# Sliding-window attention beside a GELU MLP on one core: the five channel tiles of each chunk's products added into one, not two, ahead of the logit matmuls, under a new order of pieces

## The chip, the cores and the metric

The kernel runs on one core of one Trainium2 chip. The metric is device microseconds (us) of one execution; lower is better. A core has a matrix engine (TensorE, PE in the profile, with PEld for its weight loads), a vector engine (VectorE, DVE), a scalar engine (ScalarE, ACT), GpSimd (POOL) and SyncE (SP). POOL and SP mostly issue DMA transfers here. Each engine works through its own instructions in program order; semaphores make one engine wait for another or for a transfer.

## The reference, cut to what matters

```
x  = A_x                                   # 1 x 2048 x 640, bf16
xn = layernorm(x)
q, k, v = split(xn @ wqkv)                 # 32 heads of 20 channels each
# position s looks at the 8 positions s, s-2, ..., s-14 (masked below 0)
logits = einsum("bhsd,bhswd->bhsw", q, kg) * scale
attn   = softmax(logits)
o      = einsum("bhsw,bhswd->bhsd", attn, vg)
mlp    = gelu(xn @ w1 + b1) @ w2 + b2      # hidden size 1536
out    = x + o @ wo + mlp
```

## The kernel before, in words

The 2048 positions are cut into four chunks of 512 columns, a chunk into four blocks j of 128. Activations lie with channels on the 128 partitions: 640 channels are five channel tiles of 128. The weights of q, k and v are read in strides, so that a partition holds channels of one head only in all five tiles: four partitions belong to each of the 32 heads.

For each chunk n, the steps are these. Each has a short name, a piece, which the written order uses; n is the first digit and j or an output tile the next.

- Layer norm: statistics (`st`, or `su`, `sq`, `ng` on ACT for chunks 2 and 3), `rs`, `rc`, then `xn`; transposes through PE for chunk 0 (`tp`, copied out by `tc`) and by DMA from SP for the others (`tc` there is L292).
- Projections on PE: `pj` n, which (0 q, 1 k, 2 v), tile (L336, five matmuls of 512 columns); chunk 0 has narrower ones (L349, L380, pieces `ga`, `gb`, `gd`, `ge`, `hj`). ACT copies each result out (`pc`, L400; `hc`, `gc` for chunk 0). `pad` copies 14 columns of the chunk before in front of k and v; for chunk 0 `pad01` and `pad02` are memsets on POOL (L405).
- Products q*k on DVE (`qk` n j h, L433): one instruction of 128x2560 makes, for block j, the products with four of the eight window positions (half h), for five channel tiles. They go to the SBUF tile `half`, of which there is one only, for all chunks.
- Adds of channel tiles on DVE (`pa` n j k, L465): k = 0 adds tiles 2 and 3 onto 0 and 1 (128x2048), k = 1 adds tile 1 onto 0 (128x1024). Two tiles, 0 and 4, are then left (`KEPT` is 2).
- Logits on PE (`lg`, L474): each matmul takes `head_of`, 128x32, as weights and sums the channels of each head over the partitions; the four blocks j write four groups of 32 partitions of one PSUM tile `L`. With two tiles left a chunk has 2 tiles x 2 halves x 4 blocks = 16 matmuls of 512 columns.
- Softmax: `cl` copies L to `Lb` (ACT, L486), `mask` (chunk 0), `m` and `mx` (DVE, L496 to L502), `ex` (ACT, L513, with a table load), `ss`, `ri`, `at` (DVE, L519 to L531).
- `xd` n j (SP, L548) spreads the weights of block j over the partitions by DMA. For odd chunks the target is the first half of `x_sb`, the input tile.
- Products with v (`av` n j h, DVE, L557), written into `half` again, so only after `lg` of the following chunk's logits where these were made in between; the sum of both halves (`aa`: an accumulating DMA from POOL for chunks 0 to 2, L567, an add on DVE for chunk 3, L569); two more adds (`ab`, L573, `ot`, L577).
- MLP: `f1` n_t (PE, L586) and `ge` n_t (ACT, L602), twelve each. Outputs `o` n block part (PE, L622 and L624, PSUM tiles `lo` and `hi`): parts 0 to 3 are the MLP's, part 4 is `wo` with the attention output `ot`. `oc` copies out (ACT), `od` adds to the output in DRAM (POOL, L635).
- Output base: `xp` (SP, L301) writes x to the output in DRAM: `xp0` chunk 0, `xp1` chunk 1, `xp2` chunks 2 and 3. `xb` n (POOL, L305) adds the bias b2 to chunk n there, after `xp` has landed.

The order is written out by hand as one string, `ORDER`, of these names. Walking it emits each engine's program; what stands in front of a piece on its engine runs before it. The order runs the chunks overlapped: the products q*k of chunk 1 come before the products with v of chunk 0, and so on. PE results of `f1`, `pj` and `hj` share four PSUM buffers, `psA`; a fifth waits until ACT has copied one out. A chunk's end is `ot33`, then `o334` and `ohi` on PE, two adds on DVE (`oclo`, L643, `ochi`, L652), and two stores.

Of the kernel before, what the change touches and what calls it, by code (L numbers as in the profile page):

```python
# [16 lines left out]
S, D, F, H, W, DIL = 2048, 640, 1536, 32, 8, 2  # L17
# [3 lines left out]
KT, FT = D // P, F // P  # L21
# [8 lines left out]
LASTB = S // P - 1  # L30
WARM = 10

KEPT = (2, 2, 2, 2)
BY_DMA = ((0, 1, 2, 3), (0, 1, 2, 3), (0, 1, 2, 3), ())
CUT = 2560
ACT_STATS = (2, 3)
# [1 line left out]
COLS = ((0, 2), (2, 4), (4, 5))  # L38

ORDER = """  # L40
wa ho st00a sum1 st00 rs00 rc00 neg1 sq1 xn00a tp00a wb xn00b tp00b mean1 tc00a rs01 rc01 tb b1 tc00b ga gb2 xn01 tp01
tc01a tc01b gb3 gb4 gd ge gc4 gc1 hj100 st02a st02 rs02 hc100 st03a st03 hj101 gc0 rc02 xn02 rs03 hj102 rc03 xn03
hc101 hc102 tp02 tc02 hj202 tp03 tc03 hj201 hc201 hj010 st11a hc010 st13a hc202 st12a hj012 hc012 hj112 hc112 f10_3
st11 ldx hj011 f10_9 st10a st10 st12 st13 rs1 qk011 ge0_3 rc1 xn13 pad01 qk000 qk001 tc13 ge0_9 xn12 tc12 pa000 qk010
pk hj110 hc110 hj111 hc111 hc011 qk030 qk031 qk021 pad11 xn11 f10_10 tc11 pa010 xn10 qk020 tc10 ge0_10 f10_2 ge0_2
hj200 hc200 f10_0 pa030 f10_6 f10_11 su20 ge0_6 xp2 su22 su23 pj111 pc111 ge0_0 su21 ng2 pj110 pc110 pj104 pc104 sq23
pj120 pc120 ge0_11 sq20 pj114 pc114 pj113 pc113 pa001 pa020 pa021 pj102 pc102 pa031 pa011 lg0 cl0 mask m0 hj212 hc212
pj123 pc123 mx0 ex0 pj103 pc103 pj112 pc112 ss0 ri0 pj101 pc101 pj100 pc100 qk110 qk100 ld2 ldo xb2 sq22 qk130 pj124
pc124 hj211 sq21 qk121 rs2 pj121 pc121 hj210 hc210 rc2 f10_8 qk131 hc211 f11_9 ge1_9 xp0 xn20 f10_1 ge0_1 f10_7 tc20
f11_5 xb0 qk120 xn21 tc21 qk101 ge1_5 ge0_7 xn23 tc23 ge0_8 xn22 qk111 o000 f11_8 ge1_8 pa130 at0 pa110 f11_0 ge1_0  # L50
pa100 pad12 f10_5 ge0_5 f11_3 ge1_3 f11_6 su32 tc22 pa120 pa101 xd00 f10_4 su33 pj214 pc214 pa111 su31 su30 pj210
pc210 pad21 xd02 ge0_4 pj211 pa121 ge1_6 pa131 lg1 pj200 pad02 av000 av001 aa00 pc200 ng3 sq32 sq31 sq30 av020 pc211
av021 xd01 av011 o001 pj213 pc213 pj122 pj202 pc202 av010 o002 ab00 ot00 pj204 pj212 o003 pc212 pj223 pj222 cl1 aa02
xd03 pc122 av030 av031 m1 mx1 sq33 rs3 pj201 rc3 pc204 o004 oc00 ab02 ot02 pj224 ex1 o020 aa01 aa03 ss1 ri1 xn33 at1
ab01 ot01 ab03 o021 o022 o023 o024 xp1 tc33 pc201 xn32 tc32 pc222 oc02 ot03 od02 f12_7 xd10 av101 pad22 xd12 pc223
f11_4 xn30 o030 o031 o032 o033 pc224 xd11 xn31 pj221 av100 aa10 o034 oc03 f11_2 o010 ge1_4 tc31 av120 o011 o012 o013
o014 av110 av111 aa11 ge2_7 pc221 od03 f11_7 ge1_7 pj203 pc203 ge1_2 xd13 f11_1 av131 tc30 pj311 pc311 av130 aa13
pj304 f12_3 ge2_3 pj310 pc310 pc304 ge1_1 pj302 av121 aa12 ab10 ot10 f11_10 pc302 ge1_10 pj313 pc313 qk201 qk200 pj312
pj314 ab11 ot11 qk210 pc312 oc01 od01 f13_8 ge3_8 qk211 o130 ab13 pa200 pc314 f11_11 ge1_11 qk231 f12_6 o131 ot13
qk230 xb3 f12_0 ge2_0 pj220 pc220 o132 o133 o134 oc13 pj301 pc301 pa210 ge2_6 ab12 ot12 qk221 pj300 pj324 pc300 qk220  # L60
f13_7 xb1 pc324 od13 pa211 pj303 o120 pa230 pa220 pa231 pc303 pad31 pa221 pa201 lg2 ge3_7 cl2 qk301 f12_2 m2 mx2 ex2
f13_10 f12_8 ge2_8 o121 o122 o123 od00 o124 oc12 qk310 ss2 pj320 pc320 qk311 ri2 at2 xd22 xd20 o110 o111 qk331 o112
o113 o114 oc11 od11 qk330 f13_6 ge3_6 f12_5 ge2_5 ge3_10 o100 ge2_2 qk320 pa330 qk321 pa320 f13_5 f12_4 ge3_5 pj322
f13_2 o101 ge2_4 qk300 xd21 pc322 pa321 o102 o103 o104 ge3_2 pa300 pa301 pa331 pa310 pa311 lg3 f13_3 av210 f13_9 oc10
od10 od12 av211 aa21 ge3_3 f12_10 ge2_10 xd23 av230 av200 f12_1 ge2_1 ge3_9 av231 aa23 f12_9 ge2_9 f13_1 ge3_1 f13_4
f12_11 av201 av221 ab21 ge3_4 av220 pj321 o210 o211 o212 f13_0 ot21 ge2_11 o213 o214 f13_11 cl3 m3 mx3 ex3 pad32 ss3
ri3 at3 xd32 oc21 o200 o201 pc321 o202 aa20 ab20 ot20 ab23 ot23 ge3_0 aa22 o203 o310 o204 oc20 pj323 pc323 ab22 ot22
av320 o230 o231 o232 o233 o234 od20 oc23 av321 aa32 xd30 o311 o312 od21 ab32 o220 o221 o222 o223 o224 ge3_11 xd31
av311 od23 o313 av301 av310 oc22 od22 o320 o321 o322 o323 av300 ot32 o324 oc32 aa31 ab31 ot31 o314 oc31 o300 o301 o302
xd33 od32 aa30 o330 o303 ab30 ot30 o304 av331 av330 aa33 ab33 o331 o332 o333 ot33 od31 xl o334 oclo oc30 ohi ochi ochd  # L70
od30
""".split()


# [1 line left out]
def kernel(  # L76
# [16 lines left out]
    nc = tc.nc  # L93
# [24 lines left out]
    wqkv = [wts.tile([P, KT, D], BF16, name=f"w{s}_sb") for s in "qkv"]  # L118
# [6 lines left out]
    wqkv_v = A_wqkv.rearrange("(t p) n -> p t n", p=P)  # L125
# [6 lines left out]
    def load_w(s):  # L132
        nc.sync.dma_start(wqkv[s][:], wqkv_v[:, :, s * D : (s + 1) * D])
# [2 lines left out]
    nc.vector.memset(x_sb[:, 1, 0:16], 0.0)  # L136
    nc.scalar.dma_start(x_sb[:, 1, :], x_nb[:, 1, :])
    nc.scalar.dma_start(b1_rt[0:FT, :], B_b1.rearrange("(t p) -> t p", p=P))
    load_w(0)
    load_w(1)  # L140
    load_x(2, BPC)
    load_w(2)
# [34 lines left out]
    mask = consts.tile([H, W, MW], BF16, name="mask")  # L177
# [289 lines left out]
    def do_lg(n):  # L467
        L = psL.tile([P, W, P], F32, tag="L", name="L")
        tiles["L", n] = L
        ts = {KT: range(KT), 3: (0, 1, 4), 2: (0, 4), 1: (0,)}[KEPT[n]]  # L470
        for t in ts:
# [189 lines left out]
    def piece(name, fn, *args):  # L661
        assert name not in pieces
        pieces[name] = lambda: fn(*args)
# [36 lines left out]
    for n in range(NCH):  # L700
# [27 lines left out]
        for j in range(BPC):  # L728
            for k in range({KT: 0, 3: 1, 2: 2, 1: 3}[KEPT[n]]):
                piece(f"pa{n}{j}{k}", do_pa, n, j, k)  # L730
# [57 lines left out]
```

## Time and profile before

| what | us |
|---|---|
| median of 3 runs | 207.31 (206.93 to 208.23) |
| the profiled execution, its time | 207.49 |
| its span, first to last instruction | 205.7 |
| PE busy in it | 200.8 |
| DVE busy in it | 175.4 |
| ACT busy in it | 127.7 |

The profile is of one execution. Its span leaves out 1.8 us of the execution's time (207.49 less 205.7). Busy time of PE is of pipelined matmuls that overlap: the distance from one start to the next says more. A group's row gives count, busy time, mean nanoseconds of one, and the idle time of the engine just before it with what ended it. The timeline gives start, duration, engine, line, operands, count, and in brackets the idle time before and what ended it.

### The profile page before, as it was taken

How to read it: one execution, taken by the hardware profiler on the slowest of the kernel's cores; microseconds unless marked ns; L12 is line 12 of the kernel's file. 1: busy time of each engine (PE TensorE's matmuls, PEld its weight loads, DVE VectorE, ACT ScalarE, POOL GpSimd, SP SyncE). 2: the span in 40 equal slices, each digit the busy share in tenths (PEclk: the TensorE clock that was granted, in tenths of full speed). 3: DMA queues.
4: the chain of work that ended last, by engine and by line, in shares of the span. 5: the costliest groups of instructions: out<-in, count | busy, mean ns of one | idle time of the engine just before them, and what ended most of it. 6: DMA issues, size and time to landing. Idle time of an engine off the chain costs nothing.

```text
span 205.7 us, 3262 instructions
## 1 busy us (share of the span) xinstructions
PE 200.8 (98%) x1285; PEld 112.2 (55%) x1285; DVE 175.4 (85%) x214; ACT 127.7 (62%) x242; POOL 34.4 (17%) x49
## 2 busy tenths in 40 slices
PE   7899999999999999999999999999999999999994
PEld 2797745565445555555555554555444555555552
DVE  3489999379998989949999994999979979799981
ACT  5488999899999879916466344834616854221210
POOL 2000000050000422102703303001023420311210
DMA  6999389969258599899996965018209998931244
GB/s 210 390 397 370 75 232 326 403 102 185 64 116 264 99 186 181 142 192 124 207 198 113 144 107 64 0 16 182 41 0 132 162 193 162 192 41 17 30 52 64
DMA packets 27335, 31.77 MB, mean 154 GB/s; under 512 B 9272, under 2 KB 22072, under 8 KB 27320
## 3 DMA queue, kind: packets, MB, share of 16 engines
q0 software_dynamic: 7408, 12.78, 39.4%
q1 hardware_dynamic: 19600, 18.58, 31.4%
q8 instruction: 10, 0.16, 0.3%
q10 hardware_dynamic: 312, 0.20, 0.3%
q14 instruction: 5, 0.04, 0.1%
HBM read 10.00 MB, written 7.54 MB: 85 GB/s over the span
## 4 chain that ended last, share of the span: by engine, by line
PE 95%; DMA 3%; SPq 0%; DVE 0%; issue 0%
PE lo L622 29%; PE hps L586 25%; PE pps L336 24%; PE hi L624 7%; PE gps L380 7%; DMA wq_sb<-in_A_wqkv_dram 3%; PE L L474 2%; PE gps L349 1%; PE tp L280 0%; SPq L130 0%; DVE osb L652 0%
## 5 line engine op out<-in xcount | busy, mean ns | idle before, releaser
L586 PE MATMUL hps<-xnT,w_sb 128*128 128x512 bf16 x240 | 55.6, 379 | 0.0
L433 DVE TENSOR_TENSOR half<-qT,kT 128x2560 bf16<-128x2560 bf16 x32 | 46.2, 1482 | 2.9 <-PE L L474 2.8
L622 PE MATMUL lo<-w_sb,hT 128*128 128x512 bf16 x144 | 41.3, 379 | 0.0
L586 PEld LDWEIGHTS <-w_sb 128*128 128x128 bf16 x240 | 22.9, 98 | 26.3 <-issue 0.8
L629 ACT CAST osb<-lo 128x512 bf16<-128x512 f32 x15 | 8.8, 587 | 36.8 <-PE hi L624 18.5
L624 PE MATMUL hi<-w_sb,hT 128*128 128x128 bf16 x144 | 31.5, 219 | 0.0
L602 ACT ACTIVATE hT<-hps,b1T 128x512 bf16<-128x512 f32 x36 | 24.0, 683 | 10.7 <-PE hps L586 10.7
L465 DVE TENSOR_TENSOR half<-half 128x2048 bf16<-128x2048 bf16 (+1 forms) x32 | 29.0, 952 | 0.2
L635 POOL DMA_DIRECT2D out_dram<-osb x15 | 13.6, 973 | 77.1 <-ACT osb L630 68.5
L557 DVE TENSOR_TENSOR half<-vT,x_sb 128x2560 bf16<-128x2560 bf16 x16 | 22.8, 1485 | 4.4 <-DMA x_sb<-e 3.0
L557 DVE TENSOR_TENSOR half<-vT,ax 128x2560 bf16<-128x2560 bf16 x16 | 22.8, 1485 | 2.3 <-PE L L474 1.4
L622 PEld LDWEIGHTS <-hT 128*128 128x128 bf16 x144 | 14.1, 98 | 16.8
L622 PE MATMUL lo<-wo,oT 128*128 128x512 bf16 x80 | 23.1, 379 | 0.0
L567 POOL DMA_DIRECT2D half<-half x12 | 14.3, 1195 | 48.9 <-DVE half L557 48.5
L336 PE MATMUL pps<-xnT,wv_sb 128*128 128x512 bf16 x75 | 18.5, 379 | 0.0
L336 PE MATMUL pps<-xnT,wq_sb 128*128 128x512 bf16 x75 | 18.3, 379 | 0.0
L336 PE MATMUL pps<-xnT,wk_sb 128*128 128x512 bf16 x75 | 17.7, 379 | 0.0
L624 PE MATMUL hi<-wo,oT 128*128 128x128 bf16 x80 | 16.9, 219 | 0.0
L173 ACT ACT_TABLE_LOAD x12 | 15.4, 1283 | 0.9 <-PEq L772 0.7
L624 PEld LDWEIGHTS <-hT 128*128 128x128 bf16 x144 | 14.1, 98 | 2.2
L573 DVE TENSOR_TENSOR half<-half 128x1280 bf16<-128x1280 bf16 x16 | 13.1, 820 | 1.3 <-DMA half<-half 1.2
L622 PEld LDWEIGHTS <-oT 128*128 128x128 bf16 x80 | 7.8, 98 | 9.4
(91 smaller groups left out, 263.7 us busy)
## 6 DMA issues: line engine op xcount, KB each, us to landing
half<-half POOLq DMA_DIRECT2D x12, 640.0 KB, 7.1
w_sb<-in_B_w_dram SPq DMA_DIRECT2D x4, 960.0 KB, 11.0
out_dram<-osb POOLq DMA_DIRECT2D x15, 160.0 KB, 4.0
ax<-e SPq DMA_DIRECT2D x8, 256.0 KB, 4.8
x_sb<-e SPq DMA_DIRECT2D x8, 256.0 KB, 4.8
out_dram<-b2bc POOLq DMA_DIRECT2D x3, 640.0 KB, 8.7
x_sb<-in_A_x_dram SPq DMA_DIRECT2D x1, 1280.0 KB, 12.9
out_dram<-x_sb SPq DMA_DIRECT2D x2, 640.0 KB, 8.7
```

Of the source, the lines that this page charges most:

```text
L173: nc.scalar.activation(warm[:], nc.const_aps.tensor(0.0, [P, 1], F32), func)
L336: nc.tensor.matmul(ps[:], lhsT=wqkv_p[which][:, ti, to, :], rhs=xnT[:, ti, :], start=(ti == 0), stop=(ti == KT - 1),)
L380: nc.tensor.matmul(ps[:, to - a, :], lhsT=wqkv_p[which][:, ti, to, :], rhs=tiles["xnT", 0][:, ti, pair * 2 * P : (pair + 1) * 2 * P], star ...
L433: nc.vector.tensor_tensor(out=half[:, j, h], in0=q[:, :, at].unsqueeze(1).to_broadcast([P, W // 2, KT, P]), in1=window(k, h, at), op=ALU.mult,
L465: nc.vector.tensor_tensor(out=kept, in0=kept, in1=gone, op=ALU.add)
L557: nc.vector.tensor_tensor(out=half[:, j, h], in0=window(qkv_tile(n, 2), h, cs), in1=ax_view(n)[:, j, ws, :].unsqueeze(2).to_broadcast([P, ...
L567: nc.gpsimd.dma_start(a, b, accum_op=ALU.add, max_dma_last_dim=CUT)
L586: nc.tensor.matmul(ps[:], lhsT=w1_sb[:, ti, ft * P : (ft + 1) * P], rhs=tiles["xnT", n][:, ti, :], start=(ti == 0), stop=(ti == KT - 1),)
L602: nc.scalar.activation(hT, tiles["hps", n, ft][:], ACT.Gelu_apprx_tanh, bias=b1T[:, ft : ft + 1], scale=1.0)
L622: nc.tensor.matmul(lo[:], lhsT=lhs, rhs=rhs[:, 0:CH], start=first, stop=last)
L624: nc.tensor.matmul(hi[:, 0 : D - CH], lhsT=lhs, rhs=rhs[:, CH:D], start=first, stop=last)
L635: nc.gpsimd.dma_start(rows, tiles["osb", n, bl][:], accum_op=ALU.add)
```

## The change

Each chunk keeps one channel tile instead of two: a third add (`pa` n j 2, 128x1024) adds tile 4 onto tile 0 in each block, and `lg` has 8 matmuls in place of 16. So four DVE instructions are added per chunk, 16 in all, and eight matmuls are taken away per chunk, 32 in all. All four chunks change. The whole `ORDER` string is new, with 16 names more. The load of the q weights is written as a loop of one pass and is the same transfer.

```diff
-KEPT = (2, 2, 2, 2)
+KEPT = (1, 1, 1, 1)
...
-    load_w(0)
+    for a in range(1):
+        ks = slice(a * KT // 1, (a + 1) * KT // 1)
+        nc.sync.dma_start(wqkv[0][:, ks, :], wqkv_v[:, ks, 0:D])
```

The order's core around the first three logit blocks and the end, before (-) and after (+):

```diff
-pa011 lg0 cl0 mask m0 hj212 hc212 pj123 pc123 mx0 ex0 pj103 pc103 pj112 pc112 ss0 ri0 pj101 pc101 pj100 pc100 qk110
+pa032 lg0 cl0 mask ldo xb1 xb0 pj100 pc100 m0 mx0 ex0 ss0 ri0 pj103 pj104 pc103 pj101 pc104 pc112 pc101 qk120 pj124
-xn22 qk111 o000 ... su31 su30 pj210 pc210 pad21 xd02 ... pa131 lg1 pj200 pad02 av000 av001 aa00
+xn23 tc23 o000 o001 ... f10_7 ge0_7 xp2 xb2 ... pj213 pa131 pj211 pc213 pa122 pa112 xd00 pa132 lg1 cl1 pad21 pad02 av000
-pa221 pa201 lg2 ge3_7 cl2 qk301 f12_2 m2 mx2 ex2
+pa222 pc314 pa232 lg2 cl2 qk300 qk301 m2 o122 ... qk330 ge3_8 f12_10 ge2_10 f12_2 qk331 mx2 ex2
-ex3 pad32 ss3 ri3 at3 xd32
+m3 f12_9 ge3_0 o210 o211 ab21 ot21 ge2_9 mx3 ge3_4 f13_1 av220 o212 ge3_1 o310 ex3 ss3 ri3
-ab33 o331 o332 o333 ot33 od31 xl o334
+ab33 ot33 o332 o333 xl o334
```

On the queues: SP issues `xp0` after two transposes of chunk 1, then `xp1`, `wo`, b2 and `w2`; `xp2` stands behind the transposes of chunk 2 and in front of `xd00`, `xd01` and `xd03` (before: `xp2` at 27.30 us, ahead of everything of the attention). On POOL `xb1`, `xb0` and then `xb2` stand in front of `pad02` and `aa00` (before: `xb2` and `xb0`). In chunk 0, `hj202` stands on PE in front of `tp02` and `tp03` in place of one more `hj10`, and on DVE `rc02` between the statistics of block 3.

More of the change, by code (lines that the diff above doesn't have):

```diff
@@ L40 @@
 ORDER = """
[L41 to L70, printed above, removed]
@@ L71 @@
-od30
+ho sum1 neg1 st00a st00 ldx rs00 rc00 xn00a tp00a wb wa xn00b sq1 rs01 tp00b tc00a ga mean1 tc00b gb2 rc01 xn01 tp01
+tc01b tc01a gb3 gb4 gc0 tb b1 gd ge hj100 hj102 gc4 st02a st02 st03a rs02 rc02 st03 gc1 rs03 hc100 hj202 hc202 xn02
+tp02 tc02 rc03 xn03 tp03 tc03 st13a st13 hj101 hc101 hj212 hc212 hj011 hc102 pk hc011 hj112 hc112 hj012 hc012 st12a
+st11a st11 st10a st12 st10 rs1 f10_3 ge0_3 hj110 pad01 qk000 rc1 xn12 tc12 qk001 hc110 qk011 hj111 xn13 tc13 pa000
+hj010 hc010 qk010 hc111 qk030 f10_9 ge0_9 hj201 hc201 f10_6 pad11 qk021 pa001 xn11 su22 qk031 xn10 ge0_6 hj200 f10_0
@@ new lines @@
+hc200 qk020 pa030 ge0_0 pa010 f10_11 ge0_11 xp0 f10_10 ge0_10 tc11 f10_2 su21 pa031 su23 su20 tc10 pj102 pc102 pj110
+pc110 ng2 ge0_2 pa020 pj114 pc114 pa011 sq20 xp1 pj123 pa002 sq22 pj112 pc123 pj113 pc113 pj120 sq21 pc120 pa021 pa012
+pa022 pj111 pc111 pa032 lg0 cl0 mask ldo xb1 xb0 pj100 pc100 m0 mx0 ex0 ss0 ri0 pj103 pj104 pc103 pj101 pc104 pc112
+pc101 qk120 pj124 pc124 sq23 ld2 pj121 at0 xd02 qk100 qk101 qk130 pc121 rs2 rc2 hj210 hc210 f10_1 ge0_1 f11_6 ge1_6
+qk121 f11_3 ge1_3 qk110 pa100 pa120 xn20 tc20 f10_5 ge0_5 pa101 xn21 tc21 f11_5 f10_4 ge0_4 f11_0 ge1_0 xn22 tc22
@@ new lines @@
+qk131 f10_8 ge0_8 xn23 tc23 o000 o001 su32 f11_8 ge1_8 qk111 pa121 pa110 pa102 pa130 f11_9 ge1_9 f10_7 ge0_7 xp2 xb2
+su33 su31 ge1_5 hj211 hc211 pad12 pj214 pc214 pj200 pa111 pj202 pc202 pc200 pj213 pa131 pj211 pc213 pa122 pa112 xd00
+pa132 lg1 cl1 pad21 pad02 av000 pc211 pj122 pc122 pj212 pc212 pj204 pj210 pj201 pc204 av001 av020 pj203 su30 ng3 sq33
+f11_1 aa00 av021 aa02 m1 xd01 av011 mx1 pc203 pj223 av010 aa01 ab00 ot00 xd03 av031 av030 pc201 ex1 sq31 sq32 pc210
+pj221 o002 o003 o004 ab02 oc00 ss1 pc221 ri1 sq30 rs3 rc3 pj220 o020 pj224 o021 o022 pc224 ot02 pc223 o023 o024 pc220
@@ new lines @@
+oc02 at1 aa03 xd10 pad22 od00 xd12 ab01 ot01 ab03 ot03 f11_10 av101 av100 o030 o031 xn30 tc30 xn31 o032 o033 o034 oc03
+xd13 av120 aa10 xn32 tc31 pj222 pc222 o010 o011 av121 av130 ge1_1 o012 f12_0 ge2_0 xd11 av111 av110 aa11 f11_4 ge1_4
+av131 aa13 ab10 qk201 f12_6 tc32 xn33 o013 o014 tc33 f11_2 ot10 qk200 pa200 ge2_6 pa201 ab11 qk211 f12_3 ge2_3 pj303
+ge1_10 ot11 pa202 pj302 ge1_2 qk210 ab13 od02 f11_11 ge1_11 pj300 pc300 pa210 f11_7 ot13 qk231 qk230 pj310 aa12 xb3
+pc302 pc303 f12_7 ge2_7 ab12 qk221 ot12 ge1_7 pa230 pj313 qk220 pc310 pad31 pj304 oc01 od01 pa231 pa220 pa211 pj312
@@ new lines @@
+pc312 pa221 pj301 pc301 pa212 o130 o131 o132 o133 o134 pj324 pc324 pc313 pj311 f13_8 oc13 f13_7 od13 pc311 pc304 pj314
+ge3_7 o120 o121 pa222 pc314 pa232 lg2 cl2 qk300 qk301 m2 o122 o123 o124 oc12 od12 f12_11 ge2_11 pj320 qk330 ge3_8
+f12_10 ge2_10 f12_2 qk331 mx2 ex2 f13_6 pa300 pa330 qk320 pa301 qk311 pj322 pc322 o110 o111 o112 qk310 ss2 o113 o114
+oc11 od11 f12_4 qk321 ri2 pa320 at2 xd21 pa302 o100 o101 ge2_2 pa310 o102 ge2_4 f12_5 f13_2 ge2_5 f13_5 ge3_5 pa321
+pc320 o103 o104 oc10 pa331 pa311 pa322 f12_8 xd23 ge2_8 f13_3 ge3_3 pa312 od03 pa332 lg3 av210 ge3_6 f12_1 ge3_2 av211
@@ new lines @@
+pj321 pc321 od10 f13_10 ge3_10 av230 av231 xd20 av200 av201 xd22 av221 aa21 f13_0 f13_4 ge2_1 cl3 m3 f12_9 ge3_0 o210
+o211 ab21 ot21 ge2_9 mx3 ge3_4 f13_1 av220 o212 ge3_1 o310 ex3 ss3 ri3 o330 o331 aa23 o213 o214 oc21 aa20 pj323 pc323
+o200 o201 o202 o203 ab20 ot20 o204 oc20 at3 xd31 ab23 o311 o312 ot23 aa22 ab22 ot22 o230 pad32 o231 o232 av310 od20
+av311 aa31 ab31 o233 xd32 av320 od21 o234 oc23 od23 f13_11 ge3_11 xd33 o220 o221 o222 o223 o224 oc22 f13_9 xd30 av300
+o320 o321 o322 av321 aa32 ab32 ot32 av301 ge3_9 o313 o323 o324 oc32 od22 ot31 aa30 ab30 av331 o314 oc31 o300 o301
@@ L72 @@
+av330 o302 od32 ot30 o303 o304 oc30 od31 aa33 ab33 ot33 o332 o333 xl o334 oclo ohi ochi ochd od30
 """.split()
```

## The prediction

> **What bounds the kernel now.** I read the page's first two parts, then its chain, then the groups with shapes kept apart, then DVE's waits and its timeline at the places the change touches.
>
> ```profile
> span 205.7 us, 3262 instructions
> PE 200.8 (98%) x1285; PEld 112.2 (55%) x1285; DVE 175.4 (85%) x214; ACT 127.7 (62%) x242; POOL 34.4 (17%) x49
> PE   7899999999999999999999999999999999999994
> DVE  3489999379998989949999994999979979799981
> PE 95%; DMA 3%; SPq 0%; DVE 0%; issue 0%
> ```
>
> PE is the bound: the chain that ended last is PE from the landing of the q weights (6.76 us) to the last matmul (202.96), without an idle slice. DVE, the engine that gets more work, has holes but few.
>
> ```profile
> L474 PE MATMUL L<-half,head_of 128*32 128x512 bf16 x64 | 4.3, 381 | 0.0
> L465 DVE TENSOR_TENSOR half<-half 128x2048 bf16<-128x2048 bf16 x16 | 19.3, 1219 | 0.1
> L465 DVE TENSOR_TENSOR half<-half 128x1024 bf16<-128x1024 bf16 x16 | 10.3, 684 | 0.1
> ```
>
> These three rows are what is touched: 32 of the first go, 16 of the last come.
>
> ```profile
> 36.53 1.05 PE L474 MATMUL L<-half,head_of 128*32 128x512 bf16 x16
> 37.52 0.74 PE L380 MATMUL gps<-xnT,wv_sb 128*128 128x256 bf16 x5
> ...
> 38.70 0.21 DVE L490 TENSOR_TENSOR Lb<-Lb,mask 32x128 bf16<-32x128 bf16 x1 [2.57 <-ACT Lb L486]
> 42.45 0.69 DVE L519 TENSOR_TENSOR sums<-e 128x512 f32<-128x512 bf16 x1 [1.77 <-ACT e L513]
> ...
> 84.97 0.82 DVE L573 TENSOR_TENSOR half<-half 128x1280 bf16<-128x1280 bf16 x1
> 85.82 0.49 DVE L577 TENSOR_TENSOR oT<-half 128x640 bf16<-128x640 bf16 x1
> 86.23 0.82 DVE L573 TENSOR_TENSOR half<-half 128x1280 bf16<-128x1280 bf16 x1
> 90.58 1.49 DVE L557 TENSOR_TENSOR half<-vT,x_sb 128x2560 bf16<-128x2560 bf16 x1 [3.01 <-DMA x_sb<-e]
> ```
>
> A block of 16 logit matmuls holds PE for about one us. DVE idles where a softmax has nothing beside it (2.57, 1.77) and where `xd10` is on its way (3.01). From the first product (17.40) to the end of `ot33` (199.28) the timeline's idle times sum to 16.5 of 181.9, so DVE works 165.4.
>
> ```profile
> 202.00 0.96 PE hi L624 x17
> 202.97 0.02 issue
> 202.99 0.29 DVE osb L652
> ```
>
> At the end PE starts `o331` at 198.98, nine matmuls of 0.216 ahead of `o334`, which needs `ot33` (199.28) at 200.9: DVE is 1.6 ahead there.
>
> **The change, part by part.** Everything is summed against the profiled execution: span 205.7, time 207.49, 0.18 above the median of the three runs.
>
> *Fewer logit matmuls.* Four start within 0.01 us of each other and the next four 0.21 later, so 16 take 4 x 0.21, and the step from the matmul ahead and to the one behind are together 0.2 longer than the usual 0.216. That 0.2 stays. Saved: 4 chunks x 2 groups x 0.215 = 1.7 on PE. The bounds are 0 (PE waits there anyway) and half of four blocks of 0.98, 2.0. The Trainium skill, "TensorEngine Tiling (Array Packing)", section "Tiling Modes", says that a change of the tiling mode drains the engine. By that rule the drain is paid once per block however short it is; the 0.2 agrees, and without it the sum would be 2.0.
>
> *More adds.* The added instruction's own row says 684 ns. In the timeline an add that needs the instruction just ahead starts 0.03 after its end (85.82), one that doesn't starts 0.08 before (86.23). In the new order the added adds follow others' blocks, so each takes 0.60: 16 x 0.60 = 9.6, bounds 9.6 and 16 x 0.72 = 11.5. The Trainium skill, "VectorE: DVE Perf Modes", section "The DRAIN you can't avoid", says that the next operation doesn't start until the pipe is empty, with an exception for one that isn't held. By the first half alone the sum would be 10.9, 1.3 more; 86.23 bears out the exception.
>
> *Does 9.6 fit DVE's holes?* I walk DVE along the new order with distances from start to start (`qk`, `av` 1.40; `pa` 1.14 and 0.60; `ab` 0.85, `ot` 0.41; `m` and `mx` together 1.7, `ss` and `ri` 2.4), and PE with 1.08 for five 512-column matmuls, corrected by what the same sums miss in before.
> - First product: 17.4, as before (the same statistics ahead of it). Chunk 0's adds end at 36.1 + 2.4 = 38.5. PE comes to `lg0` at 38.15 if it never waits, 38.9 with the wait below. `lg0`, `cl0`, `mask` to `mx0`, `ex0`, `ss0`, `ri0`: idle 2.1 and 1.2 (the table is loaded beside DVE), `qk120` at 46.3.
> - Chunk 1's products and adds end at 67.9. PE is at `lg1`, and `av000` starts at 68.1, against 64.86: the four adds added twice, less holes that shrank.
> - `at1` ends at 87.1; `xd10` takes its 5.5 (85.05 to 90.58 in before), so `av101` starts at 92.5, against 90.58: a hole of 3.0 is partly filled by work that comes later.
> - Chunk 2's adds end at 129.5. No wait for `lg2` any more: `qk300` needs only the block's first matmul (before: 2.83). Chunk 3's adds end at 155.2, `av210` starts at 155.8, against 152.77.
> - From there the work is as before (43.7). `ss3` doesn't wait now, since `av220` stands in front of it (1.12 before); `ab22` has its DMA issued only 5.6 ahead, against 5.9 to 8.2 from issue to landing for these, 0.9 late; `av310` waits 0.4 for `xd31`. `ot33` ends at 200.8, 1.5 later than before.
> So about 8 of the 9.6 vanish in holes, and the 1.6 of reserve at the end takes the rest, all but nothing.
>
> *New waits on PE.* PE never waited; in the new order it does, by the same walk:
> - `tp02` and `tp03` stand behind only 20 narrow matmuls (2.2 after 10.02) while `xn02` and `xn03` end at 12.3 and 13.0: 0.7.
> - `pj124` is the fifth result in `psA` behind `ex0` on ACT: ACT comes to `pc103` 4.85 after `lg0`, PE needs it after 4.3: 0.55.
> - `lg1` needs `pa132` (67.9), PE is there at 67.6: 0.3. `lg2` needs `pa232` (129.5), PE is there at 128.5: 1.0. `lg3`: none left, as PE is by then late itself.
> Sum 2.55. Each is a difference of two sums, good to some 0.5; together they lie between 0 and about 5 (each twice). Behind a waiting `lg` on PE stand `pj` and `f1`, which ACT can do without for 1 us.
>
> *Moved transfers.* `xp2` now goes out at about 60, behind `tc23`, with `xd00`, `xd01`, `xd03` behind it on SP; `xb2` waits for its landing on POOL, and `pad02` and `aa00` stand behind that. In before `xp2` landed after 5.7, another `xp` behind 3 MB of loads after 11.2. At 5.7 it lands at 66; `pad02` follows `xb2` by 0.8 and takes 0.7: 67.6, before `av000` (68.1). Charged at nothing, with 0.5 to spare; at 11.2 it costs 5.
> `xp0` ahead of two transposes of chunk 1 delays them by its issue, 0.6, and they have 1 us; nothing. `hT`, `wo` and w2 come as early as they are needed. ACT gets nothing more.
>
> *Sum.* PE: 205.7 - 1.7 + 2.55 = 206.5. DVE: 200.8 + 0.1 + 1.08 (`o334`) + 0.96 (`ohi`) = 202.9, against 202.96 in before: 205.7. PE binds by 0.8: span 206.5, time **208.3**.
>
> **The rivals.**
> 1. *PE doesn't wait.* The gain of 1.7 stays whole: span 204.0, time 205.8. For it: in before there's not one PE wait, in an order just as dense. Against it: DVE must end `ot33` by 199.2, 1.6 ahead of my walk.
> 2. *`xp2` in front (slower).* If `xp2` needs more than 6.2 from issue to landing, `pad02` comes after DVE is ready for `av000`, and chunk 0's products with v, `xd10`'s DVE partner and all behind shift by the excess. DVE has 0.8 against PE at the end. At 8.7 (the other two's middle) the excess is 2.5, at 11.2 it is 5; less 0.8 that is 1.7 or 4.2 more than the sum: 210 to 212.5. It decides for slower by 1% from an excess of 1.9. For it: `xp2` is 1120 KB, the largest store, and 768 KB of `xd` follow. Against it: nothing else is loaded at 60 us.
> 3. *The holes stay.* DVE is as often idle as in before (16.5) since each hole is an answer awaited from ACT or a DMA: `ot33` at 199.28 + 9.6 = 208.9, DVE's way to the end gives span 213.7, time 215.5; half of it 211. For it: 2.57, 1.77 and 3.01 have nothing of chunk n+1 that could run there. Against it: 2.83 and 1.12 have.
> That the change doesn't do what it says can be left out: the matmuls are counted in the program.
>
> **How the numbers follow.** A measurement of this kernel can tell about 1% (2.07) from no change: 205.24 to 209.38. My forecast, 207 to 209.4, has 0.42. Rival 1 has 0.12; a third of it lies under 205.24 (a walk that is off by 0.5 as well). Rival 2 has 0.24, rival 3, mostly half of it, 0.22; both are slower. So faster 0.04, within 1% 0.42 + 0.08 = 0.50, slower 0.46. The range takes rival 1's 205.8 and reaches to 212.5 of rival 2, leaving out some 0.08 above and below each. The forecast's own range is 207.0 to 209.4.
>
> **What would show it.** L474 x32 and L465's 1024 row x32 at 684; PE idle ahead of L280 (some 0.7), L336 (0.5) and L474 (1.3 together), nowhere else over 0.3; DVE's waits for L486 and L513 in chunk 0 some 3.3 together, none for L474 at `qk300`; `av000`, `av101`, `av210` at 68.1, 92.5 and 155.8; `ot33` at 200.8. It is wrong if the end of the chain is DVE over a stretch, if `av000` waits for POOL's L405 memset or a DMA by over 1, or if PE's idle sum is under 1.

## The result, and the profile after

The changed kernel takes 208.03 us (median; 207.44 to 211.0), the kernel before beside it 207.24 (206.93 to 208.23): ratio 1.0042, with a 95% interval of 1.0026 to 1.0057. That is inside 1%, and on the slow side of no change. A repetition gave 208.29 (207.74 to 209.15), ratio 1.0054 [1.0034, 1.0073]. The profile read here is that of the repetition, whose profiled execution took 208.29 with a span of 206.4, since the first profile of the changed kernel is of its slowest execution (211.0).

From the page of the changed kernel: span, busy time, the two engines over 40 slices, and the engines' shares of the chain that ended last.

```profile
span 206.4 us, 3216 instructions
PE 200.1 (97%) x1253; PEld 111.3 (54%) x1253; DVE 183.7 (89%) x230; ACT 128.4 (62%) x242; POOL 34.4 (17%) x49
PE   7899999999999999999999999999999999999993
DVE  2589999379999899969999999999989999899971
PE 86%; DMA 6%; ACT 3%; DVE 2%; SPq 1%; issue 0%; ACTq 0%
```

DVE works 8.3 longer (183.7 against 175.4) in a span that is 0.7 longer. PE is still the bound, but the chain is no longer PE alone: 6% of it is transfers and 3% ACT. That is how a short wait of PE shows there: by way of `tp03` the chain runs back over a load of x (7.03 us), by way of `o220` over a store (5.64).

Its groups with shapes kept apart:

```profile
L476 PE MATMUL L<-half,head_of 128*32 128x512 bf16 x32 | 2.5, 384 | 0.0
L467 DVE TENSOR_TENSOR half<-half 128x2048 bf16<-128x2048 bf16 x16 | 19.2, 1216 | 0.0
L467 DVE TENSOR_TENSOR half<-half 128x1024 bf16<-128x1024 bf16 x32 | 20.4, 686 | 0.0
```

32 logit matmuls are left, and 32 small adds of 686 ns stand where 16 of 684 stood.

Its DVE timeline at the places that the prediction named:

```profile
41.03 0.21 DVE L492 TENSOR_TENSOR Lb<-Lb,mask 32x128 bf16<-32x128 bf16 x1 [3.14 <-ACT Lb L488]
44.21 0.69 DVE L521 TENSOR_TENSOR sums<-e 128x512 f32<-128x512 bf16 x1 [1.19 <-ACT e L515]
46.59 1.43 DVE L435 TENSOR_TENSOR half<-qT,kT 128x2560 bf16<-128x2560 bf16 x1
...
65.59 2.49 DVE L467 TENSOR_TENSOR half<-half 128x1024 bf16<-128x1024 bf16 x4
68.62 5.70 DVE L559 TENSOR_TENSOR half<-vT,ax 128x2560 bf16<-128x2560 bf16 x4 [0.54 <-PE L L476]
...
91.41 2.89 DVE L559 TENSOR_TENSOR half<-vT,x_sb 128x2560 bf16<-128x2560 bf16 x2 [0.81 <-DMA x_sb<-e]
...
126.62 1.90 DVE L467 TENSOR_TENSOR half<-half 128x1024 bf16<-128x1024 bf16 x3
129.21 2.90 DVE L435 TENSOR_TENSOR half<-qT,kT 128x2560 bf16<-128x2560 bf16 x2 [0.70 <-PE L L476]
...
152.90 1.29 DVE L467 TENSOR_TENSOR half<-half 128x1024 bf16<-128x1024 bf16 x2
155.00 4.30 DVE L559 TENSOR_TENSOR half<-vT,ax 128x2560 bf16<-128x2560 bf16 x3 [0.81 <-PE L L476]
...
199.17 0.49 DVE L579 TENSOR_TENSOR oT<-half 128x640 bf16<-128x640 bf16 x1
```

The brackets give the idle time before a row. The wait for `xd10` fell from 3.01 to 0.81, the one at chunk 2's logits from 2.83 to 0.70. `ot33` ends at 199.66, only 0.38 after its end in before, although the DVE executes 16 instructions more.

Its PE timeline: the rows with a wait of over 0.2 after the first projection, the four logit blocks, and the start of `o220` (last row):

```profile
8.55 1.56 PE L351 MATMUL gps<-xnT,wq_sb 128*128 128x128 bf16 x25 [0.22 <-DVE xnT L287]
30.54 1.25 PE L338 MATMUL pps<-xnT,wq_sb 128*128 128x512 bf16 x5 [0.43 <-ACT trash L223]
39.27 0.62 PE L476 MATMUL L<-half,head_of 128*32 128x512 bf16 x8
39.82 4.51 PE L338 MATMUL pps<-xnT,wq_sb 128*128 128x512 bf16 x20
44.70 1.67 PE L338 MATMUL pps<-xnT,wv_sb 128*128 128x512 bf16 x7 [0.37 <-ACT qT L402]
68.03 0.70 PE L476 MATMUL L<-half,head_of 128*32 128x512 bf16 x8
128.71 0.61 PE L476 MATMUL L<-half,head_of 128*32 128x512 bf16 x8
154.54 0.61 PE L476 MATMUL L<-half,head_of 128*32 128x512 bf16 x8
182.70 0.38 PE L624 MATMUL lo<-w_sb,hT 128*128 128x512 bf16 x1
```

No logit block waits for the adds. The last adds of chunks 1, 2 and 3 end at 68.08, 128.52 and 154.19 (start and duration above), and PE comes to the blocks at 68.03, 128.71 and 154.54: DVE has a reserve of about 0, 0.2 and 0.35 there; ahead of chunk 0's block it has 1.4 (its adds end at 37.89, the block starts at 39.27). At 68.03 the block is 0.08 longer than the others, since its last matmuls meet the last add. The waits stand elsewhere: `gd` (8.55), `pj102` (30.54), `pj124` (44.70).

Counted from start to start, a matmul's distance over the usual one gives what PE lost: `gd` 0.35, `tp03` 0.23, `pj102` 0.60, `pj124` 0.53, `o220` 0.29 (182.70, 0.13 after the matmul ahead has ended), and 0.4 in three places of 0.1 to 0.17. Sum 2.4. From the first projection matmul to the end of the last matmul PE takes 196.19 in before and 196.90 here: 196.19 less 1.69 (measured below) plus 2.4 is 196.9. The rest of the span: PE starts 0.37 earlier, and the end after the last matmul is 0.34 longer (last section).

### The profile page after: what moved, and what is told of

It reads as the page before. It is cut to its first block, busy times and chain, and to the rows that moved or that the text cites. A ratio compares the mean times of both kernels' runs of the same rounds, so it can differ in the third digit from the quotient of the medians.

```text
span 209.1 us, 3216 instructions
## 1 busy us (share of the span) xinstructions
PE 201.4 (96%) x1253; PEld 112.0 (54%) x1253; DVE 183.8 (88%) x230; ACT 128.3 (61%) x242; POOL 34.4 (16%) x49
## 4 chain that ended last, share of the span: by engine, by line
PE 91%; DMA 4%; ACT 3%; issue 0%; DVE 0%; ACTq 0%
PE lo L624 26%; PE hps L588 24%; PE pps L338 22%; PE hi L626 7%; PE gps L382 7%; DMA out_dram<-osb 4%; PE idle L448 2%; PE L L476 1%; PE gps L351 1%; PE tp L282 1%; ACT L175 1%; ACT osb L631 1%; ACT qT L402 1%; ACT e L515 0%; ACT hT L604 0%
## 5 line engine op out<-in xcount | busy, mean ns | idle before, releaser
L467 DVE TENSOR_TENSOR half<-half 128x1024 bf16<-128x1024 bf16 (+1 forms) x48 | 38.6, 864 | 0.1
L637 POOL DMA_DIRECT2D out_dram<-osb x15 | 14.1, 984 | 70.1 <-ACT osb L632 64.4
L569 POOL DMA_DIRECT2D half<-half x12 | 15.2, 1266 | 39.9 <-DVE half L559 39.7
L338 PE MATMUL pps<-xnT,wq_sb 128*128 128x512 bf16 x75 | 17.7, 380 | 0.8 <-ACT hT L604 0.8
L307 POOL DMA_DIRECT2D out_dram<-b2bc x4 | 6.7, 1814 | 59.4 <-DMA b2bc<-in_B_b_dram 35.0
```

Of the source, the lines that this page charges most:

```text
L338: nc.tensor.matmul(ps[:], lhsT=wqkv_p[which][:, ti, to, :], rhs=xnT[:, ti, :], start=(ti == 0), stop=(ti == KT - 1),)
L467: nc.vector.tensor_tensor(out=kept, in0=kept, in1=gone, op=ALU.add)
L569: nc.gpsimd.dma_start(a, b, accum_op=ALU.add, max_dma_last_dim=CUT)
L637: nc.gpsimd.dma_start(rows, tiles["osb", n, bl][:], accum_op=ALU.add)
```

## The experiments

My theory ahead of them: PE binds; halving the logits gives about 1.7 on PE; the third adds cost nothing in the new order and much in the old; what turns the gain into a small loss is that the new order makes PE wait at places where the old one doesn't. The rivals: the adds themselves cost (DVE); or the new order is good by itself, and the one tile spoils it; and, later, that a wait that is taken away only comes back at the next piece.

**The changed kernel again.** No edit.

> The changed kernel once more, for a profile beside the ones below. My theory (waits on PE in the new order take back the 1.7 us of matmuls): 1.003 to 1.006 of before, DVE's `av000`, `av101`, `av210` near 67.8, 90.6 to 92.5 and 155.5 us, PE idle at `pj124` 0.5 and together 1 to 2.5. Rival (DVE's longer work binds the end): `ot33` later than `o333` on PE, and PE idle mostly ahead of L476 and of `o334`.

Measured: 208.29, ratio 1.0054 [1.0034, 1.0073], profile as above.

**The old order with one tile.** The kernel before, with the third adds put straight ahead of each logit block (the other chunks likewise):

```diff
-KEPT = (2, 2, 2, 2)
+KEPT = (1, 1, 1, 1)
...
-pa011 lg0
+pa011 pa002 pa022 pa032 pa012 lg0
```

> The order of before, with one channel tile kept: the four third adds of a chunk stand straight ahead of `lg`, which has 8 matmuls. Theory (the adds are hidden only where the order was made for them): in the old order PE comes to `lg` 0.4, 0, 1.7 and 0.5 us behind the last add, so 2.4 us more of adds make it wait 2.0, 2.4, 0.7 and 1.9, less 1.7 of matmuls: some 5.3 us more than before, 212.5 us, and PE idle ahead of L474. Rival (DVE's 16.5 us of holes hide the 9.6 wherever they stand): 205.5 to 207.3 us.

Measured: 211.79 (211.56 to 211.89), ratio 1.0216 [1.0196, 1.0235]. Its PE timeline around chunks 0, 1 and 3:

```profile
36.49 0.39 PE L474 MATMUL L<-half,head_of 128*32 128x512 bf16 x1
37.95 0.61 PE L474 MATMUL L<-half,head_of 128*32 128x512 bf16 x7 [1.08 <-DVE half L465]
...
65.55 0.38 PE L474 MATMUL L<-half,head_of 128*32 128x512 bf16 x1 [0.65 <-DVE half L465]
...
155.27 0.39 PE L474 MATMUL L<-half,head_of 128*32 128x512 bf16 x1 [0.66 <-DVE half L465]
156.47 0.61 PE L474 MATMUL L<-half,head_of 128*32 128x512 bf16 x7 [0.81 <-DVE half L465]
```

Without the new order PE waits inside or ahead of every block but chunk 2's; start to start it loses 1.5, 2.5, 0.1 and 1.9 (expected 2.0, 2.4, 0.7, 1.9). So in the old order the adds do cost, on PE, at the logits.

**The logits alone halved.** The kernel before with one line changed; tile 4 is left out of the logits:

```diff
-        ts = {KT: range(KT), 3: (0, 1, 4), 2: (0, 4), 1: (0,)}[KEPT[n]]
+        ts = {KT: range(KT), 3: (0, 1, 4), 2: (0,), 1: (0,)}[KEPT[n]]
```

> The kernel before with 8 logit matmuls per chunk and no third add: tile 4 is left out of the logits. It prices the matmuls alone. Theory (a group of four takes 0.21 us, and 0.2 us of each block stays however short it is): a block loses 0.43 us, four lose 1.7, time 205.5 us (205.5 to 206.2 if PE then waits for the last adds at `lg1` and `lg3`, where it has no reserve). Rival (a block halves, 0.49 each): 205.3 us, and the step around an L474 block would be half as long too. Second rival (the matmuls were no bound): 207.2 us.

Measured: 205.58 (205.53 to 205.75), ratio 0.9919 [0.9901, 0.9938], 1.6 less. PE's stretch is 194.50, against 196.19: 1.69. Its PE timeline at chunk 0's logits:

```profile
36.27 0.62 PE L474 MATMUL L<-half,head_of 128*32 128x512 bf16 x8
36.81 0.74 PE L380 MATMUL gps<-xnT,wv_sb 128*128 128x256 bf16 x5
```

From block to next matmul it is 0.55, where 16 matmuls took 0.98 (36.53 to 37.52 in before; the rows are rounded): 0.43 less a block, not half of 0.98. Four times 0.43 is 1.7.

**The new order with two tiles.** The changed kernel without its third adds and with all 16 matmuls:

```diff
-KEPT = (1, 1, 1, 1)
+KEPT = (2, 2, 2, 2)
...
-pa012 pa022 pj111 pc111 pa032 lg0
+pj111 pc111 lg0
```

> The new order with two tiles kept, that is without the 16 third adds and with all 64 logit matmuls: the order alone. Theory (part of the new waits on PE, those at the transposes and at `pj124`, come with the order and not with the adds): PE 205.7 plus 0.4 to 1.2 of waits, none at `lg`: 207.9 to 208.7 us, 1.002 to 1.006 of before. Rival (all of the loss comes from DVE's 9.6 us of adds): the order costs nothing, 207.2 us or less, PE without idle as in before.

Measured: 209.39 (208.85 to 210.57), ratio 1.0116 [1.0092, 1.0141], slower than expected. The order alone costs 2.2. In its profiled execution, the shortest of its six (208.85, span 207.0), PE's stretch is 197.67, 1.48 over that of before; the waits at `gd` 0.35, `tp03` 0.20, `pj124` 0.53, one at 83.33 us 0.21 and `o220` 0.14 make 1.43 of it. None of them has to do with the number of tiles.

**The new order, 8 matmuls, no third adds.** As the one above, with the edit of the halved logits; tile 4 is left out.

```diff
-        ts = {KT: range(KT), 3: (0, 1, 4), 2: (0, 4), 1: (0,)}[KEPT[n]]
+        ts = {KT: range(KT), 3: (0, 1, 4), 2: (0,), 1: (0,)}[KEPT[n]]
...
-pa012 pa022 pj111 pc111 pa032 lg0
+pj111 pc111 lg0
```

> The changed kernel without its 16 third adds: 8 matmuls per chunk, DVE has 9.6 us less, tile 4 is left out of the logits. Theory (the adds lie wholly in DVE's holes, and PE's waits have other causes): the same time as the changed kernel, 1.003 to 1.007 of before, DVE waiting about 2.4 us more ahead of the mask, `av000`, `qk300` and `av210`. Rival (the adds still cost something): up to 2 us less, below before's 207.2.

Measured: 208.52 (207.85 to 209.18), ratio 1.0055 [1.004, 1.0069]. Without the 16 adds it is no faster than the changed kernel with them (208.03 and 208.29). Its waits on DVE (total, times, longest):

```profile
DVE half L559 <- PE L L476: 6.2, 2, 3.2
DVE Lb L492 <- ACT Lb L488: 4.9, 1, 4.9
DVE half L435 <- PE L L476: 2.8, 1, 2.8
```

In the changed kernel the same three waits are 1.4 (0.54 and 0.81), 3.14 and 0.70. Taken away, the adds turn into waits for PE: they run in holes. The halved logits save only 0.9 here (209.39 to 208.52). Its profiled execution, the longest of its six, has a wait of more than the 0.8 that is missing, though one execution doesn't explain a median. Its PE timeline:

```profile
105.97 1.89 PE L338 MATMUL pps<-xnT,wq_sb 128*128 128x512 bf16 x8 [1.05 <-DMA xnT<-xn]
```

`pj303` waits 1.05 (1.21 from start to start) for a transpose by DMA; in the profile of the changed kernel it doesn't wait at all. This wait changes from one execution to another: in the changed kernel's execution of 211.0 it is 0.77.

The six cases together, medians in us:

| | 16 matmuls, no third add | 8 matmuls, no third add | 8 matmuls, third add |
|---|---|---|---|
| old order | 207.2 | 205.6 | 211.8 |
| new order | 209.4 | 208.5 | 208.0 to 208.3 |

The adds cost 6.2 in the old order and nothing that these runs can tell in the new one; the new order costs 2.2 to 2.9 without them. Old order against new with the adds in: 3.5 to 3.8 gained. The rival that the adds are what costs falls, and so does the one that the order is good by itself.

**A fourth add.** How much room is left? In each block of the changed kernel tile 2 is added once more, onto tile 3, which nobody reads any longer; what the kernel computes is unchanged.

```diff
+        if k == 2:
+            dead, more = (half[:, j, :, :, t : t + 1, :].rearrange("p h w t c -> p (h w) t c") for t in (3, 2))
+            nc.vector.tensor_tensor(out=dead, in0=dead, in1=more, op=ALU.add)
```

> The changed kernel with each third add followed by a further one of the same size, onto a channel tile that nobody reads any more: 16 adds, 9.6 us of DVE, the result unchanged. It asks how far the cover reaches. Theory (DVE's holes took the first 9.6, and the last add of a chunk now ends 1.3, 0.1, 0.3 and 0.3 us ahead of its `lg`): some 1.8 to 2.4 us more per chunk is waited for by PE, less the 1.3 once, 6 to 7 us in all, 213 to 215.5 us, PE idle ahead of L476. Rival (the holes that are left, 3.1, 1.2, 0.5, 0.7, 0.8 and others, cover this too): 208 to 209 us.

Measured: 214.38 (213.81 to 215.29), ratio 1.0365 [1.0343, 1.0388]. The longest of its waits on PE:

```profile
PE L L479 <- DVE half L467: 3.8, 6, 0.8
```

Where the first 16 adds cost nothing, 16 more cost 6.1 to 6.4 of their 9.6: beyond the reserves at the logits (1.4 at `lg0`, then 0, 0.2 and 0.35) little room was left, and PE waits at L479, the logits, as in the old order.

**Taking the waits away.** The waits that make the difference should go when their pieces are put elsewhere. First `pc112`, so that ACT empties the buffer that `pj124` needs before it comes to `ex0`:

```diff
-pj112 pc123 pj113 pc113
+pj112 pc123 pc112 pj113 pc113
...
-pc104 pc112 pc101
+pc104 pc101
```

> The changed kernel with the copy `pc112` moved ahead of `pc113`, so that a buffer of `psA` is free when PE comes to `pj124` during `ex0`. Theory (0.53 us of the loss is this wait): PE goes from `pj101` to `pj124` without the idle 0.37 us, and the time falls by 0.3 to 0.5 us. Rival (PE's lateness there is given back later, as DVE is behind it): the idle goes, the time stays, and a wait ahead of L476 at `lg1` takes its place.

Measured: 208.74 (207.84 to 210.77), ratio 1.0075 [1.0051, 1.0099]: no gain. Its PE timeline:

```profile
43.66 2.32 PE L338 MATMUL pps<-xnT,wv_sb 128*128 128x512 bf16 x10
...
67.61 0.59 PE L476 MATMUL L<-half,head_of 128*32 128x512 bf16 x5 [0.21 <-DVE half L467]
...
105.33 1.46 PE L338 MATMUL pps<-xnT,wq_sb 128*128 128x512 bf16 x6 [0.73 <-ACT hT L604]
```

The wait at `pj124` is gone, but PE then comes to `lg1` earlier than DVE, and waits inside the block (0.6 start to start, 0.5 more than in the changed kernel): DVE has no reserve at `lg1`, so what PE alone gains ahead of it is given back there. Set against the changed kernel's profile, PE starts `lg0` 0.51 earlier, `lg1` 1.04 earlier, and the matmul behind `lg1` 0.52 earlier: the 0.53 of `pj124` is gone again, what was gained ahead of `lg0` is kept. In this execution `pj303` waits too, though the row names ACT: the transpose that it reads landed at 105.19, and it starts at 105.33.

Then the outputs' end: `od21` in front of `od20`, so that the transfer behind which `o220` waits is out earlier.

```diff
-aa22 ab22 ot22
+aa22 od21 ab22 ot22
...
-av320 od21 o234
+av320 o234
```

> The changed kernel with the store `od21` issued ahead of `od20` on POOL, so that the buffer that `oc23` needs is free earlier; `o220` waits for `oc23` (0.29 us of PE in one profile of the changed kernel, 2.43 in another). Theory (this wait hangs on a transfer's time and makes the changed kernel's runs spread): 0.3 to 0.8 us less in the median, and a spread like that of before. Rival (DMA time differs from run to run everywhere): median and spread as those of the changed kernel.

Measured: 208.30 (207.38 to 209.23), ratio 1.0039 [1.0018, 1.0059]. The wait at `o220` isn't in its profile, which is of its shortest execution; the spread of the times and the median stay. That this wait alone makes the spread isn't borne out, though no profile shows whether its longer executions still have it.

Four at once: both of these, `tc01a` ahead of `tc01b` (for `gd`), and `xp0` behind `tc10` (for `pj102`):

```diff
-tc01b tc01a
+tc01a tc01b
...
-ge0_11 xp0 f10_10 ge0_10 tc11 f10_2 su21 pa031 su23 su20 tc10
+ge0_11 f10_10 ge0_10 tc11 f10_2 su21 pa031 su23 su20 tc10 xp0
```

> Four small moves in the new order: `pc112` ahead of `pc113`, `od21` ahead of `od20`, `tc01a` ahead of `tc01b` as in before (0.35 us of PE at `gd`), `xp0` behind `tc10` (0.6 us of PE at `pj102` in one profile). Theory (the changed kernel is 1.7 us of matmules faster and loses 2.3 us in these places): PE's waits sum to 0.5 us, time 206.0 to 206.7 us, 0.994 to 0.998 of before, faster than both. Rival (DVE binds next): what PE gains at these places it waits at `lg` and for `ot33`: 207.2 us or more.

Measured: 207.46 (207.04 to 208.4), ratio 1.0017 [1.0003, 1.0031]; the range expected is missed by 0.8. In its profile `gd` and `pj124` don't wait and `pj102` loses 0.18 instead of 0.60, but `lg1` loses 0.6, as with the first edit alone. PE's stretch is 195.67, 1.23 less than in the changed kernel's profile: PE starts `lg0` 0.92 earlier and the matmul behind `lg1` 0.93 earlier, so here too only what `pj124` gave is lost again. That it is the move of `xp0` that helps `pj102` isn't shown: in seven other profiles with `xp0` in front, `pj102` loses 0 to 0.11. From SP's queue in the changed kernel, `xp0` and the two transposes behind it:

```profile
23.15 0.53 SPq L303 DMA_DIRECT2D out_dram<-x_sb  x1
25.23 4.00 SPq L294 DMA_TRANSPOSE xnT<-xn  x2
```

SP is done with `xp0`'s issue at 23.68 and idles until 25.23, so the issue itself delays nothing there.

`o331`, the second last output, in front of `o332` instead of far ahead, so that POOL's last store goes out earlier beside the end of PE (last section):

```diff
-o330 o331 aa23
+o330 aa23
...
-ab33 ot33 o332 o333
+ab33 ot33 o331 o332 o333
```

> The changed kernel with `o331` moved behind `ot33`, where it stood before; `o304`, `oc30` and `od30` come 0.65 us earlier by it. In the profiles POOL's last wait ends 4.6 to 4.8 us after `od30` is issued, in the changed kernel 0.35 us after everything else, in the kernel before just ahead of SP's. Theory (this store sets the end of the span in the new order): the time from the last matmul to the end of the span falls from 3.1 to 2.8 us, the median by 0.3. Rival (the end is set by the last two stores): 3.1 us stays.

Measured: 207.90 (206.89 to 209.89), ratio 1.0043 [1.0022, 1.0065]. The time from the last matmul to the end of the span falls from 3.12 to 2.78, as expected; the median can't resolve it.

The four, this one, and the transposes of chunk 3 earlier (for `pj303`):

```diff
-o034 oc03 xd13 av120 aa10 xn32 tc31
+o034 xn32 oc03 xd13 av120 aa10 tc31
...
-ge1_1 o012
+ge1_1 xn33 o012
...
-tc32 xn33 o013
+tc32 o013
```

> The four moves of the mended kernel, `o331` as above, and two for the wait at `pj303`: `xn32` ahead of `oc03` and `xn33` behind `ge1_1`, so that the transposes of chunk 3 are issued 1.3 to 1.8 us earlier. Theory (the rest of the spread comes from those transposes, which land 8 us after their issue behind other transfers, on the very moment at which PE needs them): 206.6 to 207.1 us, 0.997 to 0.9995 of before, with no PE idle ahead of L338 at 105 us. Rival (DVE binds at `lg`): PE waits there by 0.5 us or more in sum, 207.2 us or more.

Measured: 208.06 (206.28 to 210.33), ratio 1.0016 [0.9987, 1.0044]. `pj303` doesn't wait in its profile (of 207.09), its transpose lands at 103.70; the spread is as wide as ever, and no theory of mine that names one wait for it is borne out.

The four and `o331`, without the transposes (of the edits shown above, all but the last):

```diff
-tc01b tc01a
+tc01a tc01b
...
-pj112 pc123 pj113 pc113
+pj112 pc123 pc112 pj113 pc113
...
-ot33 o332 o333
+ot33 o331 o332 o333
```

> The four moves and `o331` behind `ot33`, without the two of `xn32` and `xn33`. Theory (each fixed wait that was seen is out: 0.35 at `gd`, 0.53 at `pj124`, 0.35 in the tail; those on transfers differ from run to run): the fastest runs at 206.5 to 206.8 us, below any of before, the median at 206.9 to 207.3, 0.998 to 1.001 of before. Rival (what is mended is waited for at `lg1`, as DVE is just behind): the fastest runs at 207.0 as for the four moves alone.

Measured: 207.84 (206.61 to 209.01), ratio 1.0032 [1.0014, 1.005]. Its PE timeline at `lg1`:

```profile
66.77 0.42 PE L476 MATMUL L<-half,head_of 128*32 128x512 bf16 x3
67.40 0.59 PE L476 MATMUL L<-half,head_of 128*32 128x512 bf16 x5 [0.21 <-DVE half L467]
```

PE comes to `lg1` at 66.77, 1.26 earlier than in the changed kernel, and loses 0.6 there to DVE. The fastest run is as the sum of the steps says, the median isn't, and no version of the new order beat the kernel before by its median.

What stays open: the runs of the new order spread more (the middle half of the changed kernel's lies in 207.68 to 208.61, of the kernel before's in 207.13 to 207.33). The profiles show three waits that come and go, each behind a transfer. Start to start, `pj102`, `pj303` and `o220` together lose 0.11 in the execution of 207.38 (`od21` first), 0.89 in that of 208.29 (the changed kernel), 1.50 in that of 208.74 (`pc112` earlier) and 3.36 in the changed kernel's execution of 211.0, whose PE timeline has these two rows:

```profile
105.19 1.03 PE L338 MATMUL pps<-xnT,wq_sb 128*128 128x512 bf16 x4 [0.77 <-ACT hT L604]
185.25 0.38 PE L624 MATMUL lo<-w_sb,hT 128*128 128x512 bf16 x1 [2.27 <-ACT osb L631]
```

So these waits account for most of what these four executions differ by. `o220` loses nothing in the four profiles with `od21` first, 0.14 to 0.51 in six others, and 2.43 in that of 211.0. Edits at each place, alone and together, did not narrow the spread of the times. But each of these versions has one profile, and of those with `od21` first it is of an execution below the median (207.38, 207.07, 207.09 and 207.13, with medians of 208.30, 207.46, 208.06 and 207.84). What their longer executions wait for wasn't seen, and why a transfer is late in one execution and not in the next isn't settled.

## Why the prediction was right

The time (208.3 forecast, 208.03 and 208.29 measured), the bound and the mechanism came out: the adds vanish, the logits save little, and PE's new waits outweigh that. By its own steps:

- *Fewer logit matmuls, 1.7.* Right: 1.69 on PE with nothing else changed, and the step behind the block is 0.55 in the changed kernel too (39.27 to 39.82). Half of a block would have been 2.0 over four. The Trainium skill, "TensorEngine Tiling (Array Packing)", section "Tiling Modes", says that a change of the tiling mode drains the engine; a part that stays however few the matmuls agrees with that (0.55 for 8 where 0.98 was for 16), though no row shows that it is a drain.
- *More adds, 9.6, of which about 8 vanish.* Right, and a little better: `ot33` ends 0.38 later instead of 1.5, and leaving the adds out doesn't speed the kernel up. In the timeline four small adds of chunk 1 take 2.49 (65.59), three gaps of 0.60 and one duration of 0.69, as put; by the rule of the Trainium skill, "VectorE: DVE Perf Modes", section "The DRAIN you can't avoid", taken without its exception, they would have taken 4 times 0.68, 2.7. The rows bear out the exception.
- *The walk of DVE.* `qk120` 46.3 against 46.59, `av000` 68.1 against 68.62, `at1`'s end 87.1 against 87.32, all within 0.5. Then `av101` 92.5 against 91.41, chunk 2's adds 129.5 against 128.52, chunk 3's 155.2 against 154.19, `av210` 155.8 against 155.00, `ot33`'s end 200.8 against 199.66: from `xd10` on all a good 1 too late. The mis-sized term is the 5.5 for `xd10`, taken over from before: from `at1`'s end to `av101` it is 4.09 here, and the transfer lands 4.04 after its issue.
- *New waits on PE, 2.55.* The sum was right (2.4), two of its terms were not. `pj124` 0.55 against 0.53 is right, `tp02` and `tp03` 0.7 against 0.23. The failed step is `lg1` 0.3 and `lg2` 1.0: both measured at nothing, since PE was itself later at `lg1` (68.03, not 67.6) and DVE 1.0 earlier at `lg2`. In their place stand `pj102` 0.60, `gd` 0.35 and `o220` 0.29. `pj102` belongs to the step "`xp0` ahead of two transposes ... they have 1 us; nothing". That 1 us wasn't there: the last transpose landed at 30.40 and `pj102` started at 30.54, and in every other profile of the new order it starts 0.13 to 0.22 after that landing too. That `xp0` is what made the 0.60 isn't shown. SP idles for 1.5 between `xp0` and the next transpose (23.68 to 25.23), and `pj102` loses 0 to 0.11 in seven other profiles with `xp0` in front and 0.10 to 0.18 in the three with it behind; why the transpose was late in this execution stays open.
- *Sum.* PE 206.5 forecast, span 206.4. That it met so closely owes something to misses that cancel: 1.3 too much at the logits and 0.5 at `tp`, 1.2 too little at three places that the walk didn't look at and 0.4 at three small ones.

The rivals. *PE doesn't wait:* no. *The holes stay:* no, the waits for PE at the logits shrank as put; the waits at chunk 0's `mask` and sums are 4.3 together where 3.3 was said, and `qk300` waits 0.70 for the logits where none was said. *`xp2` in front* doesn't occur; from the queues of SP and of POOL in the changed kernel:

```profile
60.20 0.58 SPq L303 DMA_DIRECT2D out_dram<-x_sb  x1
```

```profile
65.01 1.28 POOL L307 DMA_DIRECT2D out_dram<-b2bc  x1 [24.36 <-DMA out_dram<-x_sb]
65.76 0.70 POOL L407 MEMSET vT<- 128x70 bf16 x1
```

`xp2` is issued at 60.20 and POOL goes on 4.8 later, earlier than the 5.7 that the step took. `pad02` ends at 66.46, 2.2 ahead of `av000`, which waits for the logits. One reading of the prediction was off without effect: in the timeline of before `o334` starts at 200.76, not 200.9, so DVE's reserve there was 1.5.

## What to carry to other kernels

An edit that moves work from the bound engine to one with holes is worth what PE saves only if the order lets the moved work into the holes, and that order has its own price: here 1.7 saved, nothing paid for 16 adds, and 2.4 paid for a handful of waits of 0.2 to 0.6 at places that have nothing to do with the adds. Look for these at every piece whose neighbour on its queue has changed, not at the edited stage alone. Where two engines meet without reserve (`lg1`), a wait that is mended for one of them alone since they last met (`pj124`, 0.53) comes back there in full; what is mended ahead of the meeting before it (`lg0`) brings both forward and is kept.

## What the runs showed of the hardware

In the changed kernel POOL's last wait sets the end of the span. For that kernel (first fence) and the one with `o331` later (second), this is the line of the kernel's end; columns are the durations in ns (min, median, max), then first and last start:

```profile
L785 POOLq DRAIN  x3: 40/93/4617, 201.0 to 206.1; - x3
```

```profile
L785 POOLq DRAIN  x3: 40/93/4753, 199.9 to 205.4; - x3
```

It begins when POOL's last store (`od30`) is issued and lasts 4.6 to 4.8 (5.1 in one profile, of the six edits), although that store lands 3.3 after its issue (201.04 to 204.32). In before `od30` went out at 200.05 and this wait ended 0.17 ahead of SP's; here it went out at 201.04 and the wait ended 0.32 after SP's (205.31), all but 0.02 of the 0.34 that the span has more at its end. So the place of the last store on POOL has a price even with PE working to the end.

The same transfer is short or long by when it goes out. What makes it so wasn't tried by itself: `xd10` landed in 4.0 to 4.3 without transposes in front of it on SP and in 5.2 in before, and the transpose of chunk 3's block 2 took 2.40 in before, where it went out at 84.04, and 7.8 to 9.6 in the new order, where it goes out at 94 to 98 among the spreads and the accumulating transfers of the attention (95.75 to 103.88 in the changed kernel).
